# Three new kinds of background step and a re-fitted table of limits in the hand-written schedule of a four-layer attention kernel

## The chip, the cores and the metric

The kernel runs on one core of one Trainium2 chip. The metric is device time in microseconds, the median of three runs; lower is better. A profile of one further execution stands beside it. The core has five engines that matter here: TensorE (PE; its weight loads are listed as PEld), VectorE (DVE), ScalarE (ACT), GpSimd (POOL) and SyncE (SP), which issues the DMAs.

## The reference, cut to what matters

Four layers run one after the other on `x` of 2048 tokens by 512 features, each on a layer norm of `x` and added to `x`. There are 32 heads of 16 features.

```python
x = x + _A_ref(_layernorm(x), ...)   # segments of 512 tokens, causal softmax, plus a memory of earlier segments
x = x + _B_ref(_layernorm(x), ...)   # full softmax attention over 2048 tokens
x = x + _A_ref(_layernorm(x), ...)
x = x + _B_ref(_layernorm(x), ...)
```

In A each of 4 segments computes `softmax(q k^T / 4 + mask) v` inside the segment, blended by a gate with `phi(q) M / (phi(q) z)`, where `M` and `z` sum `phi(k)^T v` and `phi(k)` over earlier segments. In B `softmax(q k^T / 4) v` runs over all keys. Both end with a product with `wo`. Nearly all the work is the exponential of the scores: 2 x 32 x 2048 x 2048 of them in the B layers alone.

## The kernel before, in words

**Units.** Scores are made keys by queries, 128 keys by 512 queries of one head at a time: one *bank*, the size of one of the eight banks of PSUM. A `Group` (from line 328) is one head pair's share of one query segment; `PARTS` (line 324) packs the causal blocks of A into such banks. The main loop, `attention`, takes up to three banks per *unit* (`take_banks`), and `unit` (line 1724) issues their score matmuls (32 rows of PE each, so four can run side by side), then one ACT instruction (line 1801) that takes the exponential of two or three banks at once from PSUM to `pT` in SBUF. Units alternate between two sets of three PSUM banks (`SLOTS`: 0 to 2 and 4 to 6). Two units later `pv_step` multiplies the banks with V (the *sums*), gathered in bank 7 (`SUMS`). All matmuls are recorded at line 622.

**Rings and pairs.** Bank 3 (`MISC`) is the spare one. When `ring_open` or `dx_open` allows it, a unit gives ACT only two banks and sends a third (a *ring*) or a third and a fourth (a *pair*) to VectorE, which computes the exponential in another way: line 1302 (`dx_first`) scales the scores into the bits of a bf16 number, as `uint16`; two *steps* add a constant each (`EXP_STEPS`), giving three tables, and each table is multiplied with V, so such a bank has three products on PE in place of one. Two ring banks make one built buffer, and its steps are a task, `task_dx`: on VectorE at line 1358 (one buffer) or 1391 (two neighbouring buffers at once), or on POOL at line 1373, as `pool_copy` decides. The first step goes to POOL if POOL's estimated end is at most POOL_D after VectorE's (POOL_D of 0: never), the second likewise by POOL_C. `R_PAIRS` is the number of unfinished pairs that still lets a ring open.

**Background.** Everything else is written as generators (`task_A`, `task_mem`, `task_B`, `task_out`): layer norms (lines 795, 824), projections (`proj_fm`, `proj_tm`: four matmuls into bank 3 and an eviction at line 684, or 682 on ACT), output products (line 1140), memory updates, weight loads. A projection may stop half-way (`["cont"]`) and go on after a later unit, and holds bank 3 until then. `background`, called after each unit, runs such steps by `bg_one` while credits (`cr_pe`, `cr_dve`) and the estimated lateness of VectorE (`late`, `EARLY`, `DVE_LATE`) allow; tasks are asked in the order of `make_tasks`, projections by segment. `wide` is set after layer 0's last segment; `near` counts the banks that are ready ahead (`ahead`, up to 400), `low` says that they run short.

**The table.** All of this is decided when the program is built, by estimates (`Sched.estimate`), and nothing on the chip decides. The limits are class constants (from line 445), overridden by `PLAN`, a table whose row k holds for units 20k to 20k + 19 (`STRETCH`, `set_limits`); it has rows 0 to 76.

**Order on the engines.** Each engine runs its own list in order; a wait stops all that is queued behind it on that engine.

Of the kernel before, what the change touches and what calls it, by code (L numbers as in the profile page):

```python
# [362 lines left out]
class Builder:  # L363
# [3 lines left out]
        0: dict(TAKEN_A=1, FILL_DVE=400, MASK_PE=800, PE_LOW=7, GAP=3, BG_BANK=400, QMIN=3, OPART=0, DIV_LATE=2500, PACE=2),  # L367
        1: dict(FILL_DVE=200, MASK_PE=800, GAP=1, BG_BANK=400, QMIN=3, LOW=20, POOL_QM=1, ACT1=600, R_PAIRS=2),
        2: dict(EVAC_ACT=800, NEAR=5, SLACK=350, R_NEAR=10, BACK=6, CARRY_W=400, NEARW=40, OPART=3, PAIRS=60, DIV_LATE=2500, BUSY_WAIT=0, TAKEN=0.3, DVE_LATE=800, BUSY_BACK=800, R_PAIRS=2),
        3: dict(R_LATE=1200, NEARW=40, PAIRS=999, MASK_PE=800, LEVEL=3, TAKEN=0.5, LOW=30, MARGIN=350, TAKEN_A=1, EARLY=300, OPART=3, QUAD=0, FILL=0.47, DX_BANK=900, CR_A=1200, DX_LATE=900, CARRY_W=1500, PART=3, CR_W=2200, HOLD_MAX=0, DVE_LATE=1700, FILL_DVE=100),  # L370
        4: dict(MARGIN=350, DX_BANK=900, NEAR=8, SLACK=550, EARLY=300, FILL=0.42, CR_B=1200, PART=0, NEARW=40, PAIRS=999, BUSY_WAIT=0, DX_FIN=3000, POOL_QM=1, POOL_XN=1, EVAC_ACT=800, R_NEAR=10, BACK=6, CARRY_W=1500, OPART=3, TAKEN=0.3, DVE_LATE=1700, BUSY_BACK=800, LEVEL=3, LOW=30, TAKEN_A=1, QUAD=0, CR_A=1200, DX_LATE=900, PACE=4),
        5: dict(ACT1=400, NEAR=8, TAKEN_A=1, SLACK=550, PV_SKIP=900, FILL_DVE=200, BACK=8, CR_W=1900, NEARW=20, OPART=2, TAKEN=0.4, LOW=14, DVE_LATE=800, QWAIT=8, HOLD_AT=40, PHI_LATE=0, REST=12, POOL_D=2500),
        6: dict(ACT1=400, NEAR=8, TAKEN_A=1, SLACK=550, PV_SKIP=900, FILL_DVE=200, BACK=8, CR_W=1900, NEARW=20, OPART=2, TAKEN=0.4, LOW=14, DVE_LATE=800, QWAIT=8, HOLD_AT=40, PHI_LATE=0, REST=12),
        7: dict(MARGIN=350, R_LATE=1500, DX_LATE=900, TAKEN_A=1, EARLY=300, CARRY_W=1500, PART=3, OPART=3, MASK_PE=800, GAP=3, QUAD=0, QWAIT=3, HOLD_SEGS=2, POOL_XN=1),
        8: dict(R_LATE=1200, NEARW=40, PAIRS=24, MASK_PE=800, LEVEL=3, TAKEN=0.5, LOW=30, MARGIN=350, TAKEN_A=1, EARLY=300, OPART=3, QUAD=0, FILL=0.47, DX_BANK=900, CR_A=1200, DX_LATE=900, CARRY_W=1500, PART=3, CR_W=2200, HOLD_MAX=0, DVE_LATE=1700),
        9: dict(R_LATE=1200, NEARW=40, PAIRS=24, MASK_PE=800, LEVEL=3, TAKEN=0.5, LOW=30, MARGIN=350, TAKEN_A=1, EARLY=300, OPART=3, FILL=0.47, DX_BANK=900, CR_A=1200, HOLD_SEGS=2),
        10: dict(ACT1=400, DX_BANK=700, NEAR=18, BACK=3, CR_W=1900, CR_B=1800, R_PAIRS=2, PAIRS=24, DIV_LATE=800, DVE_LATE=800, POOL_D=2500),
        11: dict(R_LATE=1500, DX_LATE=900, REST=12, NEAR=8, TAKEN_A=1, R_NEAR=50, PV_SKIP=500, FILL_DVE=400, BUSY_ROOM=900, CR_W=1300, DX_LAG=1, LOW=20, HOLD_SEGS=2, BACK=6),
        12: dict(R_LATE=1500, REST=12, NEAR=8, TAKEN_A=1, R_NEAR=50, PV_SKIP=500, FILL_DVE=400, BUSY_ROOM=900, CR_W=1300, DX_LAG=1, LOW=20, HOLD_SEGS=2, BACK=6, PHI_LATE=300),
        13: dict(R_LATE=1500, REST=12, NEAR=8, TAKEN_A=1, R_NEAR=50, PV_SKIP=500, FILL_DVE=400, BUSY_ROOM=900, CR_W=1300, DX_LAG=1, LOW=20, HOLD_SEGS=2, BACK=6, PHI_LATE=300, POOL_D=500, LEVEL=1, POOL_C=4000),  # L380
# [65 lines left out]
    MASK_PE = 500  # L446
    MASK_POOL = 2000
    PHI_LATE = 100
# [3 lines left out]
    NEARW = 60  # L452
# [15 lines left out]
    PART = 2  # L468
# [1742 lines left out]
```

## Time and profile before

| what | value |
|---|---|
| median of 3 runs | 1710.47 us (1709.43 to 1712.46) |
| profiled execution, its time | 1711.88 us |
| its span, first to last instruction | 1710.1 us |
| granted TensorE clock | 0.998 |
| ACT line 1801, instructions | 1543 |
| evictions of ring and pair banks, line 1302 | 1065, of them 107 of two banks |
| steps on VectorE, lines 1358 and 1391 | 373 and 110 (an instruction of line 1391 does two) |
| steps on POOL, line 1373 | 604 |

The span is the profile's own time; some 1.8 us lie outside it. In rows by groups the columns are line, engine, operation, tile written and tile read with shapes, count, busy us, mean ns, and the idle time of the engine before them with what ended it. In rows by windows the columns are the window, its length, then busy us and instruction count of each engine named, the granted clock, and the DMA's share and rate. Matmuls are pipelined, so a busy PE is not PE at its peak. Row k of the table begins with ACT's instruction 20k of line 1801: row 27 at 650.6 us, row 30 at 716.9, row 35 at 829.4, row 58 at 1336.2, row 60 at 1374.1, row 69 at 1546.7.

### The profile page before, as it was taken

To read this page: it belongs to the slowest core of one execution; us is meant where nothing else is said; L and a number is where in the kernel's file an instruction comes from. 1 tells how busy PE (TensorE), PEld (TensorE's weight loads), DVE (VectorE), ACT (ScalarE), POOL (GpSimd) and SP (SyncE) were. 2 spreads that over 40 slices of the span, in tenths; PEclk is the share of its full clock that TensorE was granted. 3 is DMA by queue.
4 is the path that set the end of the run, shared out by engine and by line. 5 is a ranking of instruction groups with operands and counts; after the bars stand their busy time and mean duration, and the time that the engine had idled before them with its cause. 6 is when DMAs were issued, how large, how long until landed. Compare 5 with 4: busy or idle time off the path is not lost.

```text
span 1710.1 us, 45200 instructions
## 1 busy us (share of the span) xinstructions
PE 1607.5 (94%) x19545; PEld 573.2 (34%) x19617; DVE 1456.7 (85%) x2618; ACT 1672.4 (98%) x1590; POOL 838.7 (49%) x944
## 2 busy tenths in 40 slices
PE   8899999999999999999999999999999999999999
PEld 5553435322222233423533522432222222222226
DVE  6657667988999898898688799789899999999996
ACT  8899999999999999999999999999999999999998
POOL 2323112457465464414254144435766766666765
PEclk9999999999999999999999999999999999999999
DMA  6110211000211001221321212012011100100000
GB/s 180 26 33 20 42 17 27 14 14 19 48 32 23 14 11 29 57 54 23 73 60 20 42 48 57 14 20 51 11 20 29 23 10 11 26 11 17 17 14 18
DMA packets 148424, 54.45 MB, mean 32 GB/s; under 512 B 128768, under 2 KB 147712, under 8 KB 148224
## 3 DMA queue, kind: packets, MB, share of 16 engines
q1 hardware_dynamic: 148224, 51.56, 14.2%
q8 instruction: 153, 2.51, 0.6%
q14 instruction: 47, 0.39, 0.1%
HBM read 18.88 MB, written 2.10 MB: 12 GB/s over the span
## 4 chain that ended last, share of the span: by engine, by line
ACT 60%; PE 22%; DVE 13%; POOL 2%; DMA 1%; issue 1%; another core or an unknown queue 0%; ACTq 0%; DVEq 0%; POOLq 0%
ACT pT L1801 58%; PE ps L622 22%; DVE KA L1302 2%; DVE wA L1302 1%; DVE wB L1302 1%; DVE dxt L1302 1%; ACT amem L893 1%; DVE lnst L795 1%; DVE dxt L1358 0%; DVE xn L824 0%; DMA xT<-xn 0%; POOL dxt L1373 0%; DMA phq<-amem 0%; POOL wB L1373 0%; DVE QA L1358 0%
## 5 line engine op out<-in xcount | busy, mean ns | idle before, releaser
L1801 ACT ACTIVATE pT<-ps 128x1024 bf16<-128x1024 f32 (+1 forms) x1543 | 1640.6, 1234 | 25.4 <-PE ps L622 21.0
L622 PE MATMUL ps<-qm,KB 32*128 32x512 bf16 x4096 | 563.8, 384 | 65.5 <-ACT pT L1801 48.9
L622 PE MATMUL ps<-pT,VB 128*17 128x512 bf16 x2849 | 491.5, 384 | 2.8 <-DVE wB L1302 1.2
L622 PEld LDWEIGHTS ps<-qm,KB 32*128 32x128 bf16 x4096 | 144.0, 91 | 585.1 <-ACT pT L1801 464.9
L1302 DVE TENSOR_SCALAR KA<-ps 128x512 uint16<-128x512 f32 (+1 forms) x448 | 319.1, 731 | 18.0 <-PE ps L622 15.3
L1373 POOL TENSOR_TENSOR dxt<-dxt,shift 128x512 int32<-128x512 int32 (+1 forms) x177 | 186.9, 1064 | 261.2 <-DVE dxt L1358 164.2
L1373 POOL TENSOR_TENSOR VA<-KA,shift 128x512 int32<-128x512 int32 (+1 forms) x188 | 193.9, 1040 | 182.6 <-DVE QA L1358 127.2
L1302 DVE TENSOR_SCALAR dxt<-ps 128x512 uint16<-128x512 f32 (+1 forms) x321 | 227.6, 725 | 19.6 <-PE ps L622 17.2
L622 PE MATMUL ps<-dxt,VB 128*17 128x512 bf16 x981 | 212.1, 381 | 0.1
L622 PEld LDWEIGHTS ps<-pT,VB 128*17 128x17 bf16 x2849 | 114.9, 87 | 282.9 <-issue 267.6
L1815 POOL TENSOR_SCALAR_AFFINE_SELECT pT<-pT 128x256 bf16<-128x256 bf16 (+4 forms) x146 | 74.0, 521 | 215.2 <-ACT pT L1801 215.0
L622 PE MATMUL ps<-QA,VB 128*17 128x512 bf16 x465 | 138.7, 382 | 0.4 <-POOL QA L1373 0.3
L622 PE MATMUL ps<-VA,VB 128*17 128x512 bf16 x465 | 127.9, 381 | 0.0
L1373 POOL TENSOR_TENSOR wA<-wA,shift 128x512 int32<-128x512 int32 (+1 forms) x91 | 98.5, 1088 | 53.6 <-DVE wA L1391 19.0
L622 PE MATMUL ps<-KA,VB 128*17 128x512 bf16 x465 | 119.5, 381 | 0.0
L1302 DVE TENSOR_SCALAR wA<-ps 128x512 uint16<-128x512 f32 (+1 forms) x153 | 108.3, 723 | 6.8 <-PE ps L622 6.1
L1302 DVE TENSOR_SCALAR wB<-ps 128x512 uint16<-128x512 f32 (+1 forms) x143 | 109.0, 782 | 5.4 <-PE ps L622 4.2
L1373 POOL TENSOR_TENSOR QA<-KA,shift 128x512 int32<-128x512 int32 (+1 forms) x69 | 77.5, 1129 | 66.5 <-DVE KA L1302 66.4
L622 PE MATMUL ps<-qm,KA 32*128 32x128 bf16 (+2 forms) x1536 | 97.1, 255 | 13.2 <-ACT pT L1801 10.8
L622 PE MATMUL ps<-VA,pT 128*128 128x51 bf16 (+1 forms) x2504 | 104.8, 188 | 2.1 <-DVE ob L1898 1.2
L622 PE MATMUL ps<-wB,VB 128*17 128x512 bf16 x498 | 104.5, 381 | 0.3 <-POOL wB L1373 0.2
L622 PE MATMUL ps<-woB,zero 128*32 128x512 bf16 (+1 forms) x322 | 104.3, 381 | 0.3
(173 smaller groups left out, 2166.0 us busy)
## 6 DMA issues: line engine op xcount, KB each, us to landing
wB<-in_B_wqkv_dram SPq DMA_DIRECT2D x48, 128.0 KB, 2.2
wA<-in_A_wk_dram SPq DMA_DIRECT2D x16, 128.0 KB, 2.3
wA<-in_A_wq_dram SPq DMA_DIRECT2D x16, 128.0 KB, 2.3
wA<-in_A_wv_dram SPq DMA_DIRECT2D x16, 128.0 KB, 2.3
out_dram<-x SPq DMA_DIRECT2D x8, 256.0 KB, 2.2
x<-in_A_x_dram SPq DMA_DIRECT2D x3, 512.0 KB, 10.1
wB<-in_B_wqkv_dram SPq DMA_DIRECT2D x1, 1536.0 KB, 13.1
oT<-ob SPq DMA_TRANSPOSE x63, 2.5
```

The costliest lines, as they stand in the source:

```text
L622: self.sc.add("pe", lambda e: e.matmul(out, lhsT, rhs, start=start, stop=stop, skip_group_check=True), reads=reads, banks=[(bank, "w", all ...
L795: self.op("dve", (lambda i, t: lambda e: e.bn_stats(st[:, k, i, 0:6], self.x[:, t, :]))(i, t), reads=[self.b_x[t]], writes=[bs], ns=690, p ...
L893: self.op("act", lambda e: e.activation(et, src, ACT.Exp), reads=bsrc, writes=self.b_amem, ns=1023, gap=915)
L1302: self.op("dve", lambda e: e.tensor_scalar(d, o, SCALE * LOG2E * 128, 127.0 * 128 + EXP_BIAS, op0=ALU.mult, op1=ALU.add), writes=self.b_dx ...
L1373: self.op("pool", lambda e: e.tensor_tensor(d, s, c, ALU.add), reads=src + [self.b_shift] + [first] * k, writes=dst, ns=165 + 1.75 * n, ga ...
L1801: self.sc.add("act", (lambda dst, src: lambda e: e.activation(dst, src, ACT.Exp, scale=SCALE))(dst, src), writes=self.b_pT[slot * 3 + i:sl ...
L1815: self.op("pool", (lambda blk, pat: lambda e: e.affine_select(blk, blk, pattern=pat, compare_op=ALU.is_ge, fill=0.0, base=0, channel_multi ...
```

## The change

Three new limits, each with a mechanism, and a table in which 72 of 77 rows differ.

- **HURRY** (row 30 only, 2500): `background` goes on when VectorE has neither credit nor spare time, and then picks from the tasks other than `task_dx`; such a step may be issued while VectorE is estimated up to 2500 ns late.
- **SPARE** (row 60 only, 20): when fewer than 20 banks are ahead, a task with matmuls is ready and no ring or pair opens, `lend_bank` keeps a unit at two banks and lends its third PSUM bank to a projection; it stays lent until that projection's last matmul.
- **ORD** (row 27: 23; rows 58, 69, 70: 3): `sort_tasks` re-orders the tasks while the row holds, moving a B layer's projections against the A layer's.
- **FIT=3** (rows 7 and 35): an existing limit; its second bit runs background steps with matmuls between a unit's scores and the sums.
- In the rest of the table limits of all kinds go up and down. R_PAIRS is 2 in 52 rows (41 before). POOL_D above 1 stands in 37 rows (20 before). POOL_D above 1 together with POOL_C of 1500 or more stands in rows 4, 15, 16, 17, 34 to 37, 40, 41, 45, 48, 53 to 56, 58, 70, 74 and 76 (before: 13, 35, 36, 37, 51, 58 and 76). Rows 1 and 2 get PE_LOW=7 and PE_A=6, rows 6 and 7 PE_A=6, row 0 DX_LATE=1700.

```diff
@@ -364,83 +364,83 @@
-        30: dict(ACT1=200, DX_LATE=700, NEAR=10, PV_SKIP=200, EARLY=500, FILL=0.53, CR_B=1800, CARRY_W=1500, OPART=3, DIV_LATE=800, DVE_LATE=800, BG_BANK=100, QUAD=0, LN1_AT=6, FILL_DVE=400, R_LATE=2200, POOL_C=2000, BACK=8, SLACK=250),
...
+        30: dict(ACT1=200, DX_LATE=700, NEAR=10, PV_SKIP=200, EARLY=500, FILL=0.53, CR_B=1800, CARRY_W=1500, OPART=0, DIV_LATE=800, BG_BANK=100, QUAD=0, LN1_AT=6, FILL_DVE=400, R_LATE=2200, POOL_C=0, BACK=8, SLACK=250, REST=4, PAIRS=60, RATE=2, HURRY=2500),
...
-        60: dict(ACT1=300, DX_LATE=900, DX_BANK=700, REST=8, NEAR=3, PV_SKIP=900, BUSY_ROOM=900, FILL=0.47, CR_B=1800, CR_A=1700, PART=3, R_PAIRS=2, NEARW=90, OPART=3, MASK_PE=200, LOW=20, DVE_LATE=800, QWAIT=3, QMIN=4, BACK=2, MARGIN=400),
...
+        60: dict(ACT1=300, DX_LATE=900, DX_BANK=700, REST=8, NEAR=3, PV_SKIP=900, BUSY_ROOM=900, FILL=0.47, CR_B=1800, CR_A=1700, PART=3, R_PAIRS=2, NEARW=90, OPART=3, MASK_PE=200, LOW=20, DVE_LATE=800, QWAIT=3, QMIN=4, BACK=2, MARGIN=400, SPARE=20, PHI_LATE=300),
...
@@ -460,6 +460,10 @@
     PACE = 0
+    SPARE = 0
+    ORD = 0
+    HURRY = 0
+    half_bank = None
...
@@ -699,6 +703,8 @@
     def misc(self):
         pool = self.misc_banks
+        if not self.bubble:
+            return min((self.banks[i] for i in pool), key=self.wait_of)
...
@@ -864,6 +870,7 @@
         bank, al = self.misc(), self.new_alloc()
+        self.half_bank = bank
...
@@ -871,12 +878,14 @@
                          [bw[ci]] + self.b_xT[slot], al)
+        self.half_bank = None
...
     def proj_tm(self, w, bw, off, slot, ti, evac, need=()):
...
         bank, al = self.misc(), self.new_alloc()
+        self.half_bank = bank
...
@@ -884,6 +893,7 @@
                          [bw[ci], self.b_xT[slot][ti]], al)
+        self.half_bank = None
...
@@ -1129,6 +1139,7 @@
             bank, al = self.misc(), self.new_alloc()
+            self.half_bank = bank
...
@@ -1137,6 +1148,7 @@
                 self.mm_wide(bank, a[:, ti * 128:(ti + 1) * 128], wo[:, c, :], n == 0, n == len(srcs) - 1, list(ba) + [bwo], al)
+            self.half_bank = None
...
@@ -1429,7 +1441,7 @@
     def bank_late(self, now=None):
...
-        return self.wait_of(self.misc_bank) - (self.sc.t["pe"] if now is None else now)
+        return min(self.wait_of(self.banks[i]) for i in ([self.misc_bank.idx] if self.bubble else self.misc_banks)) - (self.sc.t["pe"] if now is None else now)
...
@@ -1467,11 +1479,11 @@
-    def bg_one(self, slack=None, bank=None):
+    def bg_one(self, slack=None, bank=None, poor=False):
...
         pick = None
-        if bank is not True and (self.gap > 1 and self.step % 2 or self.dx_urgent()):
+        if bank is not True and not poor and (self.gap > 1 and self.step % 2 or self.dx_urgent()):
...
@@ -1486,11 +1498,11 @@
                 pick = task
-        if pick is None and bank is not True:
+        if pick is None and bank is not True and not poor:
             pick = self.dx_next()
-        if pick is None or (slack is not None and pick["next"][2] > 0 and self.cr_dve + slack < pick["next"][2] and self.late("dve") > self.EARLY):
+        if pick is None or (slack is not None and pick["next"][2] > 0 and self.cr_dve + slack < pick["next"][2] and self.late("dve") > (self.EARLY if pick in self.dx_tasks else max(self.EARLY, self.HURRY))):
             return False
-        if slack is not None and not pick["next"][1] and (pick["next"][2] or not self.PACE) and self.late("dve") > (self.DVE_LATE_LOW if self.low else self.DVE_LATE if not self.ends(1) else self.DVE_FIN):
+        if slack is not None and not pick["next"][1] and (pick["next"][2] or not self.PACE) and self.late("dve") > max(self.DVE_LATE_LOW if self.low else self.DVE_LATE if not self.ends(1) else self.DVE_FIN, 0 if pick in self.dx_tasks else self.HURRY):
...
@@ -1521,8 +1533,9 @@
     def background(self, bank=None):
-        while (self.cr_dve > 0 or self.late("dve") < self.EARLY) and (self.cr_pe > 0 or self.FIT and self.wide and not self.low):
-            if not self.bg_one(self.SLACK, bank):
+        while self.cr_pe > 0 or self.FIT and self.wide and not self.low:
+            poor = not (self.cr_dve > 0 or self.late("dve") < self.EARLY)
+            if poor and not self.HURRY or not self.bg_one(self.SLACK, bank, poor):
...
@@ -1538,10 +1551,16 @@
                     order.append((-5, self.task_out(B, s)))
+        self.first_key = {base * 100 + s * 10 + (13 if base or s > 1 else 5): base * 100 + s * 10 for base in (0, 2) for s in range(4)}
...
         order += [(1000, self.task_dx())]
-        self.tasks = [{"gen": g, "next": next(g)} for _, g in order]
+        self.tasks = [{"gen": g, "next": next(g), "key": k} for k, g in order]
...
+    def sort_tasks(self):
...
+        move = lambda k: self.first_key.get(k, k - self.ORD) + self.ORD
+        self.tasks.sort(key=lambda t: (move(t["key"]), t["key"]) if self.ORD else (t["key"], 0))
...
@@ -1721,9 +1740,18 @@
-    def unit(self, n, items, dx):
+    def lend_bank(self, n, pair):
...
+        bank = self.slot(n)[2 - 2 * (n % 2)]
+        if bank is self.half_bank:
+            return bank
+        if not n or self.bubble or pair or self.near >= self.SPARE:
+            return None
+        return bank if any(t["next"][1] > 0 and self.met(t["next"][0]) for t in self.tasks) else None
...
+    def unit(self, n, items, dx, lent=None):
         pair7 = len(dx) == 2 and self.misc_bank.idx == SUMS
-        u = self.slot(n)[1 if dx and n % 2 and not pair7 else 0:]
+        u = self.slot(n)[1 if (dx and not pair7 or lent is not None) and n % 2 else 0:]
...
@@ -2077,6 +2105,7 @@
         self.stretch = -1
+        self.ordered = 0
...
@@ -2089,12 +2118,18 @@
                 self.set_limits(self.stretch)
+                if self.ORD != self.ordered:
+                    self.sort_tasks()
+                    self.ordered = self.ORD
...
                 self.step -= 1
-            items = self.take_banks(2 if pair else 3)
+            lent = self.lend_bank(n, pair)
+            if lent is not None and lent is self.half_bank:
+                pair = 0
+            items = self.take_banks(2 if pair or lent is not None else 3)
...
@@ -2111,7 +2146,7 @@
                 continue
-            self.misc_banks = [self.misc_bank.idx]
+            self.misc_banks = [self.misc_bank.idx] + ([lent.idx] if lent is not None else [])
...
@@ -2124,7 +2159,7 @@
             dx = []
-            while len(items) == 2 and len(dx) < pair:
+            while len(items) == 2 and lent is None and len(dx) < pair:
...
@@ -2134,7 +2169,7 @@
                     self.ring_step = self.step
-            elif pair:
+            elif pair and lent is None:
...
@@ -2142,7 +2177,7 @@
                 items += self.take_banks(3 - len(items))
-            self.unit(n, items, dx)
+            self.unit(n, items, dx, lent)
```

More of the change, by code (lines that the diff above doesn't have):

```diff
@@ L366 @@
     PLAN = {
[L367 to L370, printed above, removed]
@@ L444 @@
+        76: dict(DX_LATE=700, REST=8, SLACK=700, R_NEAR=20, R_PAIRS=2, NEARW=90, PAIRS=999, LEVEL=1, LOW=14, GAP=1, DVE_LATE=800, BG_BANK=400, QUAD=0, POOL_WAIT=300, PV_SKIP=100, BACK=6, FILL=0.47, PART=0, LN1_AT=3, EARLY=300, DIV_LATE=2500, MARGIN=400, POOL_C=4000, ACT1=300, MASK_PE=200, POOL_D=2500, BUSY_ROOM=300, CR_W=1500, TAKEN=0.5, POOL_XN=1, CR_A=1700, CR_LOW=2000),
     }
```

135 lines of the change are left out of this document (69 added, 66 removed).

## Prediction

> **What bounds the kernel now.** I read the busy times first, then the chain, then ACT's instructions by form, then busy times by stage.
>
> ```profile
> PE 1607.5 (94%) x19545; PEld 573.2 (34%) x19617; DVE 1456.7 (85%) x2618; ACT 1672.4 (98%) x1590; POOL 838.7 (49%) x944
> ```
> ```profile
> ACT 60%; PE 22%; DVE 13%; POOL 2%; DMA 1%; issue 1%; another core or an unknown queue 0%; ACTq 0%; DVEq 0%; POOLq 0%
> ```
> ```profile
> L1801 ACT ACTIVATE pT<-ps 128x1024 bf16<-128x1024 f32 x1065 | 1016.5, 1114 | 8.5 <-PE ps L622 5.8
> L1801 ACT ACTIVATE pT<-ps 128x1536 bf16<-128x1536 f32 x478 | 680.6, 1501 | 16.9 <-PE ps L622 15.2
> ```
> ACT is busy 1672.4 of 1710.1 us, almost all of it in the exponentials of line 1801, which wait only 25.4 us in all. So the kernel ends earlier only if ACT gets fewer score banks (or if the first stage starts ACT sooner). 1065 units have two banks on ACT and 478 have three: 3564 banks. A two-bank unit sends its third bank through VectorE (line 1302), whose steps then run on VectorE (1358, 1391) or POOL (1373). In all 3564 + 1065 + 107 (the wide forms of line 1302 take two) = 4736 banks are fixed by the reference and the masks.
>
> What is a bank worth? I compare a stretch of two-bank units with one that is nearly all three-bank:
>
> ```profile
> 945.00:975.00 30.00, 26.90 (x22) 1.00 0.14 28
> 1604.20:1641.00 36.80, 36.54 (x41) 1.00 0.06 12
> ```
> These are ACT's line 1801 alone. The upper window holds 20 units in 26.9 us (one of two banks), the lower 40 units in 36.5: 1.35 and 0.91 us a unit, with the instructions cut at the edges counted into the 22 and 41. **A bank taken off ACT is worth about 0.41 us** (1501 - 1114 gives 0.39, 1.35 - 0.91 gives 0.44).
>
> Who limits how many banks leave ACT? The stages, each row PE, PEld, DVE, ACT, POOL:
>
> ```profile
> 0.00:300.30 300.30, 272.15 (x3893) 134.95 (x3928) 205.64 (x476) 281.01 (x231) 72.14 (x130) 0.99 0.22 50
> 300.30:611.80 311.50, 295.99 (x3230) 87.37 (x3234) 280.20 (x462) 307.90 (x301) 180.04 (x191) 1.00 0.12 23
> 611.80:801.30 189.50, 178.84 (x2137) 60.50 (x2138) 167.17 (x321) 188.68 (x184) 77.06 (x94) 1.00 0.16 36
> 801.30:1217.10 415.80, 394.64 (x5060) 152.54 (x5080) 343.84 (x653) 409.29 (x372) 185.27 (x213) 1.00 0.19 41
> 1217.10:1710.10 493.00, 465.87 (x5241) 137.84 (x5241) 459.79 (x710) 485.48 (x509) 324.24 (x317) 1.00 0.08 18
> ```
> VectorE is at 90% in the second stage, 93% in the last, but 88% and 83% between. POOL is nowhere over 66%. So where rings are dense VectorE is nearly used up while POOL has room.
>
> **The change, part by part.** Its three new kinds of step hardly run; the table does.
>
> *Lending a bank* needs SPARE, which only row 60 has (units 1200 to 1219, 1374 to 1393 us now), and fewer than 20 banks ahead. *ORD* stands in rows 27, 58, 69 and 70.
>
> ```profile
> L684 DVE CAST KB<-ps x32: 675/691/693, 113.4 to 1219.6; 128x512 bf16<-128x512 f32 x32
> L684 DVE CAST QB<-ps x32: 658/691/692, 115.6 to 1230.2; 128x512 bf16<-128x512 f32 x32
> ```
> The last K and Q projections are done at 1219.6 and 1230.2 us. From then on every group's inputs exist, so 343 units' banks are ahead at row 60, and lending never opens; and in rows 58, 69 and 70 no projection is left whose place ORD could change. In row 27 (651 to 671 us) it puts layer 3's first projection behind layer 2's third segment, which matters only if layer 2's first segment is already through; the order is put back 20 units later. I cost these at zero, and at 2 us either way if the stages have moved. The new `misc()` chooses among one bank outside the start, so zero as well.
>
> *HURRY* stands in row 30, *FIT=3* in 7 and 35 (in 7 it changes nothing, since steps sit between scores and sums there anyway until `wide`).
>
> ```profile
> 716.90:737.10 20.20, 19.07 (x212) 5.52 (x213) 18.45 (x37) 20.20 (x21) 7.57 (x8) 1.00 0.18 51
> 829.40:855.70 26.30, 25.30 (x321) 11.38 (x321) 20.13 (x36) 25.76 (x24) 7.64 (x7) 1.00 0.26 42
> ```
> ACT is busy all 20.20 us of row 30, so HURRY has no idle time to take back; a projection half whose eviction queues up to 2.5 us behind VectorE's other work holds the spare bank, and nobody else needs it in those 2.5 us except a ring. Bounds -1 to +2.5 us, taken as zero. Row 35 has 0.54 us in which ACT is idle; FIT=3 can win that and can lose about as much by putting matmuls ahead of the sums. Zero.
>
> *The early rows* 0 to 2, 6 and 7 give more background work to a unit (PE_LOW 7, PE_A 6).
>
> ```profile
> ACT pT L1801 <- PE ps L622: 10.7, 19, 1.9
> ```
> That is ACT's wait for scores in the first 142.5 us. More projection work per unit brings the next segment sooner and delays these scores; -3 to +5 us, taken as zero.
>
> *The other limits.* 72 of 77 rows change. Two kinds have a direction that can be counted. R_PAIRS is 2 in 52 rows, in 41 before, which lets a ring open with one more pair unfinished. And both steps of a built pair may go to POOL: POOL_D above 1 (first step) together with POOL_C of 1500 or more (second) stands in 20 rows after and 7 before, 13 more. What this does is seen in rows 35 to 37, which have both now, against rows 61 to 63, which have not. In turn for POOL's steps, VectorE's and VectorE's double ones:
>
> ```profile
> 829.40:900.20 70.80, 30.27 (x28) 1.00 0.24 52
> 1392.70:1450.30 57.60, 29.55 (x29) 1.00 0.05 11
> ```
> ```profile
> 829.40:900.20 70.80, 1.66 (x3) 1.00 0.24 52
> 1392.70:1450.30 57.60, 5.85 (x9) 1.00 0.05 11
> ```
> ```profile
> 1392.70:1450.30 57.60, 9.04 (x12) 1.00 0.05 11
> ```
> POOL takes 28 of 31 steps in the first window, 29 of 29 + 9 + 2 x 12 = 62 in the second: 90% against 47%. A row has some 62 / 3 = 21 steps there, 10 in the first window; at 15 a row, 13 more rows move 13 x 15 x 0.43 = 84 steps.
>
> ```profile
> L1358 DVE TENSOR_SCALAR QA<-KA x112: 278/420/1257, 322.4 to 1694.5; 128x1024 uint16<-128x1024 uint16 x107, 128x512 uint16<-128x512 uint16 x5
> ```
> ```profile
> L1373 POOL TENSOR_TENSOR VA<-KA,shift x188: 611/1038/1489, 312.3 to 1696.4; 128x512 int32<-128x512 int32 x181, 128x256 int32<-128x256 int32 x7
> ```
> ```profile
> L1302 DVE TENSOR_SCALAR KA<-ps 128x512 uint16<-128x512 f32 x406 | 269.7, 681 | 14.9 <-PE ps L622 12.2
> ```
> Each frees 0.42 us of VectorE (35 us) and costs POOL 1.04 (87 us, off the path while POOL keeps up: 838.7 + 87 is 54% of the span). A further bank on VectorE costs it 0.68 for the eviction and about 0.12 for its share of the steps, so 35 us pay for 44 banks, 18 us of ACT. Not all comes back: of the added rows those in the second and last stages (15 to 17, 53 to 56, 70, 74) sit where VectorE limits; the others (4, 34, 40, 41, 45, 48) mostly where it had time left. I take somewhat under half: **20 banks, 8 us**. The rest of the table has no sign that I can read from the trace, zero, with 5 us either way.
>
> The sum: 1711.9 us, the profiled execution (span 1710.1 and 1.8 around it), less 8 is 1703.9. The median of the runs is 1710.5, 1.4 lower, so **1702.5 us** as a median.
>
> **The rivals.**
>
> *Slower: POOL's steps lock VectorE out.* The same work on VectorE's SBUF-to-SBUF steps, next to a POOL step and alone:
>
> ```profile
> 704.03 1.04 POOL L1373 TENSOR_TENSOR wB<-wB,shift 128x512 int32<-128x512 int32 x1
> ```
> ```profile
> 704.09 1.26 DVE L1358 TENSOR_SCALAR QA<-KA 128x1024 uint16<-128x1024 uint16 x1
> 705.27 0.41 DVE L1358 TENSOR_SCALAR VA<-KA 128x1024 uint16<-128x1024 uint16 x1
> ```
> The one that began 0.06 us after POOL's took 1.26 us and the next 0.41: it stood still until POOL was done, 0.85 us lost. The Trainium skill, SBUF — State Buffer, section "SBUF: two separate sides", states the rule: the pair of ports that VectorE and GpSimd share is an exclusive lock held for a whole instruction, and the loser blocks; by that rule every step moved can cost VectorE more than it frees, and the trace's 1.26 agrees that the block is whole. The mechanism decides once a moved step costs VectorE over 0.42 us by blocking others. At 0.65 (between 0.42 and 0.85) VectorE loses 84 x 0.23 = 19 us net, 24 banks go back to ACT, +10 us: **1720 us**. Against it:
>
> ```profile
> 1217.10:1710.10 493.00, 67.56 (x121) 1.00 0.08 18
> ```
> ```profile
> 1217.10:1710.10 493.00, 286.46 (x274) 1.00 0.08 18
> ```
> In the last stage 121 single steps on VectorE (upper row) took 67.56 us, 18 more than at 0.41 each, beside 274 POOL steps (lower row): 0.07 us lost for each, far under 0.42. But other VectorE work without PSUM is blocked too, and a reordered table shifts more than these.
>
> *No difference.* The freed VectorE time falls where rings are kept shut by something else (the spare bank is held by a projection, or PE), or one stretch gives back what another wins. This is also the case in which the change does not do what its name says. 1710 us.
>
> *Much faster.* The limits open rings in the middle stages:
>
> ```profile
> L1801 ACT ACTIVATE pT<-ps 128x1024 bf16<-128x1024 f32 x231 | 221.2, 1095 | 3.1 <-PE ps L622 2.5
> ```
> ```profile
> L1801 ACT ACTIVATE pT<-ps 128x1024 bf16<-128x1024 f32 x214 | 207.4, 1062 | 4.1 <-PE ps L622 2.9
> ```
> Two-bank units of the second stage (231 of its 301) and of the fourth (214 of 362). At 18 and 15 of 20 they would be 271 and 272: 98 banks, 40 us; half of that, 20 us, gives **1690 us**. For it: VectorE's 17% of idle time in the fourth stage. Against it: PE is busy 394.6 of 415.8 us there, and a bank on VectorE needs three products with V instead of one, and the spare bank is shared with the projections.
>
> **How the numbers follow.** Forecast 0.52, much faster 0.18, no difference 0.08, slower 0.22. The forecast's own spread, from the zeros with bounds, is 1697 to 1707. The range leaves out half of the much-faster case and somewhat under half of the slower one: 1689 to 1718. Faster by over 0.2% (3.4 us, about what a measurement of this kernel can tell from no change) 0.70, within 0.08, slower 0.22.
>
> **What would show it.** Right: more than 1065 two-bank units (about 1085), POOL busy by about 80 us more, steps of lines 1358 and 1391 fewer by some 80, evictions of line 1302 more by 20, VectorE's share still near 85%, ACT's wait before line 1801 near 25 us. Wrong: the same number of two-bank units with a different time (then it is ACT's waits or the first stage), or mean durations of line 1358 well above 0.51 us with fewer rings (the lock). No unit with two banks on ACT and no bank on VectorE means that lending never ran. If the early stage moves by more than 5 us, my zero for it was wrong.

## The result and the profile after

The kernel after takes **1706.2 us** (median of 20 runs, 1702.1 to 1711.0), the kernel before beside it 1710.3 us (20 runs, 1708.1 to 1713.0): a ratio of **0.9977, 95% interval 0.9968 to 0.9987**. The change makes the kernel about 4 us faster, half of the 8 us that were forecast. The profiled execution of after took 1705.5 us with a span of 1703.8.

From here on lines of the score and sum matmuls are 626 in after (622 before), the exponentials 1829 (1801), ring evictions 1314 (1302), VectorE's steps 1370 and 1403 (1358, 1391), POOL's steps 1385 (1373). The kernels of the experiments have lines of their own.

First the page of after: busy times, and the shares of the chain.

```profile
PE 1603.3 (94%) x19699; PEld 570.6 (33%) x19699; DVE 1472.4 (86%) x2555; ACT 1656.1 (97%) x1574; POOL 966.7 (57%) x1057
...
ACT 53%; PE 26%; DVE 16%; POOL 3%; issue 1%; DMA 0%; ACTq 0%; SPq 0%; POOLq 0%; DVEq 0%
```
ACT is busy 16.3 us less than before, but the span is only 6.3 us shorter: ACT's idle time went from 37.7 to 47.7 us. The chain spends less of the span on ACT (60% before) and more on PE and VectorE (22% and 13%). VectorE, which the change was to relieve, is busier than before.

ACT's exponentials by form:

```profile
L1829 ACT ACTIVATE pT<-ps 128x1024 bf16<-128x1024 f32 x1064 | 1016.4, 1098 | 16.9 <-PE ps L626 14.6
L1829 ACT ACTIVATE pT<-ps 128x1536 bf16<-128x1536 f32 x465 | 660.6, 1503 | 18.8 <-PE ps L626 16.9
```
There are as many two-bank units as before (1064 for 1065), but 13 fewer units of three banks: ACT takes 2 x 1064 + 3 x 465 = 3523 banks, 41 fewer. They left by pairs: 1529 units hold 4736 banks, so 4736 - 3523 - 1064 = 149 units sent a fourth bank to VectorE, against 107. The wait ahead of the exponentials grew from 25.4 to 35.7 us, in both forms.

The first and the last stage (columns as in the prediction's table of stages):

```profile
0.00:300.30 300.30, 273.43 (x3963) 133.30 (x3964) 207.07 (x470) 285.01 (x234) 82.05 (x141) 1.00 0.22 50
...
1217.10:1703.80 486.70, 460.94 (x5235) 139.11 (x5232) 453.23 (x651) 470.88 (x484) 375.21 (x364) 0.99 0.09 18
```
In the first 300.3 us ACT is busy 285.0 us for 281.0, 4.0 us more. So the account of the two profiled executions is: 16.3 us of ACT work removed, 4.0 us of idle time won at the start, and 14.0 us of new idle time later. Not all of the 4.0 is the change's: the trace of before grants PE half the clock twice in this stage, for 3.4 us each at 44 and 68 us, the trace of after not once. In two later runs with before's plan and no such window there (e6 and e10) ACT is busy 283.5 and 283.4 us, so the change's own part is 1.5 us or less.

Who holds up the weight loads, which come ahead of every matmul (columns: who waits for whom, us in total, times, longest):

```profile
PEld ps L626 <- DVE KA L1314: 20.7, 46, 1.6
PEld ps L626 <- DVE dxt L1314: 18.6, 44, 0.9
PEld ps L626 <- DVE wA L1314: 9.8, 20, 1.2
...
PEld ps L626 <- DVE wB L1314: 8.0, 18, 0.9
```
The same in before:

```profile
PEld ps L622 <- DVE KA L1302: 14.0, 37, 1.2
PEld ps L622 <- DVE dxt L1302: 12.7, 32, 1.0
PEld ps L622 <- DVE wB L1302: 7.0, 16, 1.0
PEld ps L622 <- DVE wA L1302: 5.8, 16, 0.7
```
57.1 us on ring and pair evictions; before it was 39.5. So the new waits are for VectorE, and the timeline shows how one arises:

```profile
809.20 2.17 POOL L1385 TENSOR_TENSOR dxt<-dxt,shift 128x512 int32<-128x512 int32 x2 [0.96 <-DVE dxt L1314]
...
809.39 1.00 DVE L1025 TENSOR_TENSOR Mn<-M,hmask 128x128 bf16<-128x128 f32 x1
...
810.42 1.10 DVE L1025 TENSOR_TENSOR Mn<-M,hmask 128x128 bf16<-128x128 f32 x1
...
811.51 0.68 DVE L1314 TENSOR_SCALAR KA<-ps 128x512 uint16<-128x512 f32 x1
812.12 0.28 DVE L1025 TENSOR_TENSOR Mn<-M,hmask 128x128 bf16<-128x128 f32 x1
...
812.25 0.38 PE L626 MATMUL ps<-qm,KB 32*128 32x512 bf16 x1 [1.18 <-DVE KA L1314]
...
813.53 1.02 ACT L1829 ACTIVATE pT<-ps 128x1024 bf16<-128x1024 f32 x1 [1.40 <-PE ps L626]
```
The same small VectorE operation takes 0.28 us alone and 1.00 and 1.10 beside two POOL steps. The eviction behind it comes late, PE waits 1.18 us for the bank, and ACT then stands idle for 1.40. Both inputs of that operation lie in SBUF; the Trainium skill, SBUF — State Buffer, section "SBUF: two separate sides", names such an operation, against a GpSimd one that reads SBUF, as a case of the lock on the shared ports, and this timeline agrees. The place is easy to read, but most of the time that VectorE loses beside POOL is lost by other operations, as e7 shows.

### The profile page after: what moved, and what is told of

It is laid out like the page before. It is cut to its first block, busy times and chain, and to the rows that moved or that the text cites. A ratio compares the mean times of both kernels' runs of the same rounds, so it can differ in the third digit from the quotient of the medians.

```text
span 1703.8 us, 45449 instructions
## 1 busy us (share of the span) xinstructions
PE 1603.3 (94%) x19699; PEld 570.6 (33%) x19699; DVE 1472.4 (86%) x2555; ACT 1656.1 (97%) x1574; POOL 966.7 (57%) x1057
## 4 chain that ended last, share of the span: by engine, by line
ACT 53%; PE 26%; DVE 16%; POOL 3%; issue 1%; DMA 0%; ACTq 0%; SPq 0%; POOLq 0%; DVEq 0%
ACT pT L1829 52%; PE ps L626 25%; DVE KA L1314 3%; DVE dxt L1314 3%; DVE wA L1314 1%; DVE wB L1314 1%; ACT amem L903 1%; DVE dxt L1370 1%; POOL dxt L1385 1%; DVE lnst L801 1%; POOL QA L1385 1%; DVE x L1152 0%; DVE xn L830 0%; DVE wB L1403 0%; POOL pT L1843 0%
## 5 line engine op out<-in xcount | busy, mean ns | idle before, releaser
L1385 POOL TENSOR_TENSOR dxt<-dxt,shift 128x512 int32<-128x512 int32 (+1 forms) x237 | 252.3, 1074 | 244.1 <-DVE dxt L1370 128.7
L1314 DVE TENSOR_SCALAR KA<-ps 128x512 uint16<-128x512 f32 (+1 forms) x424 | 310.9, 753 | 16.8 <-PE ps L626 15.1
L1314 DVE TENSOR_SCALAR dxt<-ps 128x512 uint16<-128x512 f32 (+1 forms) x341 | 249.8, 749 | 18.4 <-PE ps L626 17.0
L626 PE MATMUL ps<-dxt,VB 128*17 128x512 bf16 x1089 | 235.7, 382 | 0.2 <-POOL dxt L1385 0.2
L1843 POOL TENSOR_SCALAR_AFFINE_SELECT pT<-pT 128x512 bf16<-128x512 bf16 (+4 forms) x134 | 73.9, 563 | 222.7 <-ACT pT L1829 222.7
L1385 POOL TENSOR_TENSOR QA<-KA,shift 128x512 int32<-128x512 int32 (+1 forms) x109 | 119.9, 1107 | 65.6 <-DVE KA L1314 62.4
L1385 POOL TENSOR_TENSOR wB<-wB,shift 128x512 int32<-128x512 int32 (+1 forms) x105 | 110.1, 1059 | 43.9 <-DVE wB L1370 17.8
L626 PE MATMUL ps<-wA,VB 128*17 128x512 bf16 x486 | 113.0, 384 | 0.3 <-POOL wA L1385 0.2
L626 PE MATMUL ps<-wB,VB 128*17 128x512 bf16 x519 | 112.5, 390 | 0.1
L626 PE MATMUL ps<-qm,KA 32*128 32x128 bf16 (+2 forms) x1536 | 95.3, 254 | 13.7 <-ACT pT L1829 10.1
## 6 DMA issues: line engine op xcount, KB each, us to landing
wB<-in_B_wqkv_dram SPq DMA_DIRECT2D x1, 1536.0 KB, 12.8
```

The costliest lines, as they stand in the source:

```text
L626: self.sc.add("pe", lambda e: e.matmul(out, lhsT, rhs, start=start, stop=stop, skip_group_check=True), reads=reads, banks=[(bank, "w", all ...
L1314: self.op("dve", lambda e: e.tensor_scalar(d, o, SCALE * LOG2E * 128, 127.0 * 128 + EXP_BIAS, op0=ALU.mult, op1=ALU.add), writes=self.b_dx ...
L1385: self.op("pool", lambda e: e.tensor_tensor(d, s, c, ALU.add), reads=src + [self.b_shift] + [first] * k, writes=dst, ns=165 + 1.75 * n, ga ...
L1843: self.op("pool", (lambda blk, pat: lambda e: e.affine_select(blk, blk, pattern=pat, compare_op=ALU.is_ge, fill=0.0, base=0, channel_multi ...
```

## The experiments

Two theories stood at first. **R**: VectorE's relief by POOL is what gained, and POOL itself is what took most of it back, by the way of VectorE. **C**: the missing part is TensorE's clock, since the trace of after shows three windows of 3.4 us at a granted clock of 0.50, at 512, 1284 and 1304 us (before has two, at 44 and 68). The second, with the stretch ahead of it (columns as in the table of stages):

```profile
1280.00:1283.00 3.00, 2.39 (x18) 0.64 (x16) 2.60 (x4) 3.00 (x5) 2.92 (x4) 1.00 0.21 42
1283.00:1287.60 4.60, 4.32 (x41) 0.96 (x41) 3.23 (x7) 3.36 (x5) 4.44 (x6) 0.63 0.16 32
```
The granted clock (third figure from the end) is 0.63 over these 4.6 us, which reach a little beyond the window. Theory R was narrowed from run to run, and each expectation says in which form it is meant. In all runs but e4 the plan is held: the same units and banks in the same order, and only what the diff names differs.

**e1, more work for PE in its gaps.** 161 short matmuls more, to keep the clock up.

```diff
-        while room > 64 / 2.4 and sc.activity(at) < self.GAP_FILL:
+        while room > 64 / 2.4 and (sc.activity(at) < self.GAP_FILL or sc.activity(at) + self.surplus < 0.78):
```


> The changed kernel with its plan frozen (same units, banks, steps and waits) and 161 more filler matmuls in PE's estimated gaps, so that fewer windows run at half clock. Theory C (half-clock windows of 3.4 us, three of them in the profile after, cost about 1.4 us per 0.001 of mean granted clock): clock 0.999 to 1.0, median 1702 to 1704 us, ACT's wait before the exponentials down from 35.7 to about 30 us. Rival (the windows are a symptom, the spread has another cause): 1706 us as before, or slower by the fillers' own time.

Measured: 1707.7 us (ratio to before 0.9989, 0.998 to 0.9999), mean clock 0.9966 over its 12 runs, the same as after's. Half-clock windows stayed, at other places. The remedy failed, so this run neither proves nor clears the clock.

**e2, before with 80 steps moved to POOL; e3, after with 103 moved back.** Both in the 15 rows in which the change newly lets both steps go to POOL.

```diff
+    def to_pool(self, k):
+        return self.stretch in (4, 15, 16, 17, 34, 40, 41, 45, 48, 53, 54, 55, 56, 70, 74)
```
```diff
+    def to_dve(self, k):
+        return self.stretch in (4, 15, 16, 17, 34, 40, 41, 45, 48, 53, 54, 55, 56, 70, 74) and k == 0
```


> The kernel before, plan frozen, with 80 single steps of the rows that the change gives POOL both steps in executed on POOL instead of VectorE; no bank leaves ACT. Theory R (the relief pays only through banks that leave ACT): VectorE's busy time down by about 30 us, POOL's up by 85, time within 2 us of 1710. The slower rival of the prediction (POOL's steps lock VectorE out): slower by 5 to 19 us, mean of the steps left on VectorE well above 0.51 us.

> The changed kernel, plan frozen, with the 103 first steps of the 15 added rows executed on VectorE again. Theory R (POOL's relief is what lets 41 banks leave ACT): VectorE 43 us busier, its evictions late, ACT's wait up, 8 to 20 us slower than the changed kernel (1714 to 1726). Rival (the gain is the first stage, 6 us by bank 400, and POOL's part is worth nothing): within 3 us of 1706, or faster because the lock is gone.

Measured: e2 1723.6 us (1.0078, 1.0066 to 1.009), 13 us slower than before. VectorE fell to 1433.9 us, but no bank was moved to it for that, so only the price is seen. The price came by POOL's queue: weight loads waited 24.5 us in all for POOL, 13.5 in before, while the steps left on VectorE (128x1024) took 539 ns, 534 before. So the form of R that expected no price missed, and the time is the slower rival's, but not by its sign.

e3 1725.2 us (1.009, 1.0077 to 1.0103), 19 us slower than after; VectorE rose to 1501.1 us:

```profile
PEld ps L658 <- DVE KA L1346: 30.1, 62, 1.6
PEld ps L658 <- DVE dxt L1346: 22.3, 50, 1.8
PEld ps L658 <- DVE wA L1346: 13.7, 27, 1.4
PEld ps L658 <- DVE wB L1346: 11.3, 25, 1.4
```
77.4 us on evictions for 57.1. Without POOL's larger share the banks of after are carried only with these waits, and after is then slower than before: that half of R holds.

**e4, one limit alone.** HURRY is taken out of row 30, everything else of the change stays.

```diff
-...REST=4, PAIRS=60, RATE=2, HURRY=2500),
+...REST=4, PAIRS=60, RATE=2),
```


> The changed kernel without HURRY in row 30, nothing else edited; the rows behind it then meet other states. The prediction's step (HURRY is worth -1 to +2.5 us): 1705 to 1709 us. Rival F (each row is fitted to the state that the rows before it leave, so any change of path costs far more than the edit itself): the profile up to row 30 is the same, then fewer banks leave ACT or ACT waits longer, 20 us or more slower.

Measured: 1740.5 us (1.0179, 1.0165 to 1.0192). This isn't HURRY's worth. Up to row 30 the units are as in after; behind it the plan is another, 17 banks come back to ACT (3540 for 3523), and ACT's wait ahead of the exponentials is 56.3 us for 35.7. The rows behind row 30 fit the state in which it leaves the plan, as rival F said, so single rows can't be priced one by one.

**e5 and e6, evictions ahead of small VectorE work.** A ring or pair eviction passes up to two operations queued ahead of it that have no part in PSUM, where it depends on none of them and its bank is estimated ready (154 places in after, 144 in before).

```diff
+            if op.ring:
...
+                while i and i > len(new) - HOPS and new[i - 1].raw and place[id(new[i - 1])] > known and ready < new[i - 1].end - new[i - 1].ns + EARLIER:
+                    i -= 1
+            new.insert(i, op)
```


> The changed kernel with its plan as it is (same units, same banks, same steps on the same engines); only the order within VectorE's queue differs: in 154 places an eviction of a ring or pair bank stands one or two places earlier, ahead of operations that read and write SBUF alone. Theory R (what the change gained on ScalarE, 16 us, was given back as 10 us of waiting, because evictions stand in VectorE's queue behind small operations that POOL's longer use makes slow): PE's waits on the evictions fall from 57 us towards 45 or less, ScalarE's wait before the exp line from 35.7 to 30 or less, time 1699 to 1704. Theory C (the waiting comes from half-clock windows of TensorE): the order changes nothing, 1704 to 1708 at a granted clock of 0.996 to 0.998. A third: the passed operations (norms, masks, maps) are what PE waits for next, and the time is 1706 to 1712.

> The kernel before, plan as it is, with the same reordering of VectorE's queue in 144 places. Theory R: the waits on evictions are 39.5 us here, so there is less to gain than in the changed kernel: 1706 to 1710. Theory C: 1708 to 1712, no change. Third: 1711 to 1716.

Measured: e5 1707.6 us (0.9983, 0.9974 to 0.9992), e6 1711.1 us (1.0008, 0.9999 to 1.0017). In e5 the waits on evictions fell from 57.1 to 52.0 us, not to 45, and ACT's wait ahead of the exponentials stayed at 35.6. As far as these places reach, the order in VectorE's queue isn't the cause; R in this form fell.

**e7 and e8, POOL's steps cut short.** 16 columns in place of 512 or 256; TensorE reads the first table three times, so the exponential's other two tables are left out of the result.

```diff
-        self.op("pool", lambda e: e.tensor_tensor(d, s, c, ALU.add), ...
+        self.op("pool", lambda e: e.tensor_tensor(d[:, 0:16], s[:, 0:16], bcast(self.shift[:, k:k + 1], [[0, 16]]), ALU.add), ...
...
-        self.pv(g, what, r, self.dx_buf(slot, k)[:, 512 * i:512 * i + 512]...
+        self.pv(g, what, r, self.dx_buf(slot, 0)[:, 512 * i:512 * i + 512]...
```


> The changed kernel with its plan as it is (same units, banks, steps, engines, orders and waits), with every POOL step cut from 256 or 512 columns to 16; TensorE reads the first table in place of the two later ones, so the output leaves out the exponent's last two tables. It prices POOL's steps: VectorE's lengthening beside them and tables or qm that come late from POOL. Theory R, in its form with POOL as the cause (the waits that the change added come from VectorE's operations that stretch beside POOL's steps, and from POOL's queue): 1688 to 1698, ScalarE's wait before the exp line under 28, and the gain against the changed kernel is larger than the same cut gives the kernel before. Theory P (TensorE is simply full in four-bank units): 1703 to 1707, wait still 33 to 37.

> The kernel before with the same cut of POOL's steps. Theory R: 1702 to 1707, ScalarE's wait 18 to 22: it gains about half of what the changed kernel gains, since it has 604 steps against 722 and 39 us of waits on evictions against 57. Theory P: 1708 to 1711, wait 24 to 26.

Measured: after falls to **1677.4 us**, before to **1698.2 us** (the unchanged kernel before, run beside them, 1709.9). By their intervals each is good to about 3 us. The pages of e7 and e8, and e7's exponentials by form:

```profile
PE 1579.4 (94%) x19699; PEld 560.5 (33%) x19699; DVE 1403.2 (84%) x2555; ACT 1648.4 (98%) x1574; POOL 372.0 (22%) x1057
```
```profile
PE 1603.2 (94%) x19617; PEld 567.3 (33%) x19617; DVE 1406.8 (83%) x2618; ACT 1668.3 (98%) x1590; POOL 341.1 (20%) x944
```
```profile
L1872 ACT ACTIVATE pT<-ps 128x1024 bf16<-128x1024 f32 x1064 | 1014.7, 1146 | 2.2 <-PE ps L658 1.2
L1872 ACT ACTIVATE pT<-ps 128x1536 bf16<-128x1536 f32 x465 | 664.7, 1515 | 11.5 <-PE ps L658 10.0
```
This is the account that was missing (the trace of before has 603 steps on POOL, not the 604 of the table ahead):

| | before | after |
|---|---|---|
| POOL's steps | 603 | 722 |
| VectorE busy, steps in full length, us | 1456.7 | 1472.4 |
| VectorE busy, steps short, us | 1406.8 | 1403.2 |
| VectorE stretched by them, us | 49.9 | 69.2 |
| time, steps in full length, us | 1709.9 | 1706.2 |
| time, steps short, us | 1698.2 | 1677.4 |
| price of POOL's steps, us | 11.7 | 28.8 |

What the change does apart from this is worth 1698.2 - 1677.4 = 20.8 us, and 28.8 - 11.7 = 17.1 us of it go to a dearer POOL. With short steps PE is as full as ever (94%), and yet ACT's wait ahead of the exponentials falls to 13.7 us, for 35.7, so a full PE isn't the cause. (Of the 28.6 us by which the spans of after and e7 differ, 20.9 are idle time of ACT and 7.7 busy time; why its busy time falls no run shows.) The weight loads' waits for evictions fall to 27.8 us in e7 (24.1 in e8):

```profile
PEld ps L658 <- DVE dxt L1346: 10.1, 28, 0.6
...
PEld ps L658 <- DVE KA L1346: 7.6, 21, 0.5
PEld ps L658 <- DVE wA L1346: 5.3, 13, 0.9
PEld ps L658 <- DVE wB L1346: 4.8, 12, 0.9
```
Which operations stretch is seen by comparing after with e7, VectorE's groups:

```profile
L1314 DVE TENSOR_SCALAR KA<-ps 128x512 uint16<-128x512 f32 (+1 forms) x424 | 310.9, 753 | 16.8 <-PE ps L626 15.1
...
L1370 DVE TENSOR_SCALAR dxt<-dxt 128x1024 uint16<-128x1024 uint16 (+1 forms) x117 | 67.6, 586 | 1.5
```
```profile
L1346 DVE TENSOR_SCALAR KA<-ps 128x512 uint16<-128x512 f32 (+1 forms) x424 | 313.8, 756 | 28.2 <-PE ps L658 25.6
...
L1402 DVE TENSOR_SCALAR dxt<-dxt 128x1024 uint16<-128x1024 uint16 (+1 forms) x117 | 48.6, 423 | 1.5
```
The evictions from PSUM take 753 and 756 ns, so they aren't touched; the steps from SBUF to SBUF take 586 beside POOL's steps and 423 without. Of 79 us by which VectorE's durations differ in sum, 59 lie in these steps (those of 128x1024 and 128x2048), 9 in the 128x512 bf16 TENSOR_SCALAR and only 1.5 in the small operation of the timeline above.

Short steps also end the waits for tables that come late from POOL, and the clock was higher (a mean of 0.9990 in e7's four runs, against 0.9966). So one more pair.

**e9 and e10, late tables taken away alone.** POOL's steps have their full length, but TensorE reads the first table and doesn't wait for them (the other two tables are left out of the result).

```diff
-                    if w is op or w.eng == "pe" and e == "pe" and not w.is_dma:
+                    if w is op or w.eng == "pe" and e == "pe" and not w.is_dma or e == "pe" and w.step:
```


> The changed kernel with its plan as it is and POOL's steps in full length, but TensorE reads the first table in place of the two later ones and doesn't wait for POOL's steps; the output leaves out the exponent's last two tables. It separates the two ways in which POOL's steps can cost the 28.8 us that cutting them short gave back: by tables that come late from POOL, or by VectorE's operations that stretch beside them. Late tables: most of the 28.8 us comes back, 1677 to 1688, while VectorE stays at 1472 us of busy time. Stretch (VectorE 1472 against 1403 us with short steps): little comes back, 1699 to 1706, at most the 7 us that weight loads wait for POOL's tables; ScalarE's wait before the exp line stays over 28.

> The kernel before with the same: TensorE reads the first table and doesn't wait for POOL's steps. Cutting the steps short gave back 11.7 us here. Late tables: 1698 to 1703. Stretch (VectorE 1457 against 1407 us): 1705 to 1710, at most the 5 us that weight loads wait for POOL's tables.

Measured: e9 1708.6 us (0.9987, 0.9976 to 0.9999), e10 1712.8 us (1.0011, 1.0003 to 1.002). Nothing came back in either; VectorE stood at 1471.4 us in e9, and the weight loads still waited for it:

```profile
PEld ps L658 <- DVE KA L1346: 20.5, 51, 1.6
PEld ps L658 <- DVE dxt L1346: 19.2, 46, 0.9
...
```
With the other two rows they are 60.1 us. Late tables are out, and so is POOL's other work (masks and the like): weight loads waited 12.8 us for it in after and 12.3 in e7. Of the ways in which POOL's steps could cost 28.8 us, two are left: the stretch of VectorE, and the clock, which was as low in e9 (a mean of 0.9959) as in after.

**e11, each POOL step in two halves.** The whole computation; each step is now two shorter instructions.

```diff
+        h = n // PIECES
+        c = bcast(self.shift[:, k:k + 1], [[0, h]])
+
+        def pieces(e):
+            return [e.tensor_tensor(d[:, i * h:i * h + h], s[:, i * h:i * h + h], c, ALU.add) for i in range(PIECES)][-1]
```


> The changed kernel with its plan as it is and the whole computation; every POOL step is issued as two instructions of half the columns (128x256 int32 took 0.61 to 0.67 us in the profiled run, 128x512 1.07 to 1.11), so that what VectorE can be held up at one stroke is halved, and POOL is busy some 90 to 120 us longer. Stretch, if an operation of VectorE waits for the end of the POOL instruction that is under way: what it loses goes with the count times the square of the duration, 2 x 0.63 squared against 1.08 squared, so 69 us of stretch become about 47, VectorE falls from 1472 towards 1450, and about a third of the 28.8 us comes back: 1694 to 1702. Rival: the stretch goes with POOL's busy time, however it is cut: VectorE stays at 1472 or rises to 1480, time 1706 to 1714.

Measured: 1729.6 us (1.0119, 1.0102 to 1.0136): slower, outside both expectations. The page and the waits of the weight loads:

```profile
PE 1603.7 (93%) x19630; PEld 572.7 (33%) x19699; DVE 1459.9 (85%) x2555; ACT 1658.7 (96%) x1574; POOL 1084.1 (63%) x1779
```
```profile
PEld ps L627 <- POOL dxt L1390: 16.9, 24, 1.4
...
PEld ps L627 <- POOL wA L1390: 10.5, 15, 1.7
PEld ps L627 <- POOL wB L1390: 10.3, 12, 2.6
...
PEld ps L627 <- POOL VA L1390: 8.1, 14, 1.2
...
PEld ps L627 <- POOL QA L1390: 5.8, 15, 0.9
```
The stretch did shrink, from 69 to 57 us, about half of what was expected. But POOL became 117 us busier, and where its queue was full its tables came late: 51.6 us of waits for 7.0. Stretch by stretch of 20 units the trace shows both signs: 33 to 36 (POOL busy 24 to 68% in after) took 2.8 us less than in after, while 15, 71 and 75 (74 to 99%) took 8.9 us more.

**e12, halves only where POOL has room.** As e11, in 15 stretches. They were picked by the result of e11: those that were shorter there than in after and left POOL room.

```diff
+SPLIT = {10, 11, 18, 26, 27, 33, 34, 35, 36, 43, 44, 46, 50, 60, 65}
...
+        m = 2 if self.stretch in SPLIT else 1
```


> The changed kernel, whole computation and plan as it is; POOL's steps are issued in two halves only in the 15 stretches of 20 units (some 127 of 722 steps) in which splitting all of them shortened the stretch and left POOL room: 10, 11, 18, 26, 27, 33 to 36, 43, 44, 46, 50, 60 and 65. In the run that split every step these 15 together took 7.0 us less than in the changed kernel's profiled run, while the stretches with POOL busy over 85% lost more than that. Stretch at one stroke, with POOL's queue as the limit where it is full: 1698 to 1703, weight loads waiting for POOL's tables under 12 us. Rival: the 7.0 us were pauses shifted from one stretch to the next, and come back in the stretches after: 1704 to 1709.

Measured: **1700.1 us** (five runs, 1699.2 to 1700.6; 0.9939, 0.9925 to 0.9952), faster than both kernels. The page, the exponentials by form, and the place of the timeline above:

```profile
PE 1591.7 (94%) x19630; PEld 568.9 (34%) x19699; DVE 1461.0 (86%) x2555; ACT 1655.3 (97%) x1574; POOL 992.3 (58%) x1186
```
```profile
L1836 ACT ACTIVATE pT<-ps 128x1024 bf16<-128x1024 f32 x1064 | 1015.4, 1097 | 12.8 <-PE ps L627 10.7
L1836 ACT ACTIVATE pT<-ps 128x1536 bf16<-128x1536 f32 x465 | 660.3, 1502 | 16.5 <-PE ps L627 14.6
```
```profile
807.66 2.50 POOL L1391 TENSOR_TENSOR dxt<-dxt,shift 128x256 int32<-128x256 int32 x4 [0.21 <-DVE dxt L1315]
...
807.85 0.57 DVE L1026 TENSOR_TENSOR Mn<-M,hmask 128x128 bf16<-128x128 f32 x1
...
809.53 0.68 DVE L1315 TENSOR_SCALAR KA<-ps 128x512 uint16<-128x512 f32 x1
...
810.27 0.39 PE L627 MATMUL ps<-qm,KB 32*128 32x512 bf16 x1 [0.61 <-DVE KA L1315]
...
811.55 1.94 ACT L1836 ACTIVATE pT<-ps 128x1024 bf16<-128x1024 f32 x2 [0.83 <-PE ps L627]
```
VectorE is busy 11.4 us less than in after, and ACT's wait ahead of the exponentials falls from 35.7 to 29.3 us. At the place shown the operation that took 1.00 us takes 0.57, PE waits 0.61 us for 1.18 and ACT 0.83 for 1.40. In the profiled runs the 15 stretches took 5.1 us less than in after and the other 62 together 0.8 less, so the pauses weren't shifted but gone. VectorE's part lies in the same 15 stretches: there it is busy 295.4 us for 305.2, in the others 1165.5 for 1167.2. In e11, where the others were split too, VectorE was busy 1165.4 us in them and POOL 892.2 for 800.5: there the halves cost POOL time and freed next to nothing.

## Why the prediction was right, and where it wasn't

Faster was right, and the time lies 3.7 us from the forecast, within the range. That it came so near is in part luck: the sum behind it was wrong in two terms that partly cancel, twice the banks and a price of POOL's steps that it put at nothing.

- **ACT bounds, a bank is worth 0.41 us.** Right: 41 banks took 16.3 us off ACT's busy time, 0.40 each. With short steps the two kernels differ by 20.8 us, of which 41 x 0.41 = 16.8 are banks.
- **Steps moved to POOL.** Well sized. VectorE's step instructions fell from 373 + 2 x 110 to 328 + 2 x 93 steps, 79 fewer, for 84 forecast. POOL got 119 more, since the added banks bring steps of their own, and 128 us, for 87.
- **"I take somewhat under half: 20 banks, 8 us."** This step failed in size: the change took 41 banks, close to the 44 that the freed time pays for. The cut for rows "where it had time left" wasn't needed. They also went by another way than the signs named: pairs, with the number of two-bank units unchanged. That sign, which I had put down as one of a wrong forecast, says nothing about how many banks leave; the count of banks does.
- **The lock.** This rival didn't decide, but it was priced in the wrong coin. VectorE lost 19.3 us more for 119 more steps, 0.16 us a step, well under the 0.42 that I gave as the point at which it decides. As lost VectorE time that would be 19.3 / 0.80 = 24 banks, 10 us; and the forecast had no term for it at all. POOL's steps cost 17.1 us more than before, not as banks (those stayed off ACT) but as waits: an eviction that comes late holds up PE, and PE holds up ACT, as at 809 us. Some 3 of the 17.1 go with the clock (below). "ACT's wait before line 1801 near 25 us" failed by this: 35.7.
- **VectorE's share near 85%** came out at 86, but the 19 us of stretch are in it. With short steps it is 3.6 us below that of before.
- **SPARE, ORD and `misc()` at zero.** Right: with ORD and SPARE taken out of the table the program is the same, instruction for instruction and wait for wait. The spare-bank and re-ordering code never acts.
- **HURRY and FIT at zero.** In row 7 FIT changes nothing, as forecast: the program without it is the same. HURRY and row 35's FIT do change the program, and their worth stays open, since e4 shows that a row can't be taken out alone.
- **The early rows at zero, -3 to +5.** Near enough. The start won 4.0 us between the two profiled executions, under the 5 us at which the zero was to count as wrong, and 1.5 us or less where neither has a half-clock window. (Which sign of -3 to +5 means a gain isn't said.) ACT's wait for scores in the first 142.5 us fell from 10.7 to 7.6, and it is 8.8 in e6 and 8.4 in e10:

```profile
ACT pT L1829 <- PE ps L626: 7.6, 18, 1.8
```
- **No difference, much faster.** Neither came. PE, which I held against the much faster case, isn't what stopped it: the same units at the same 94% ran in 1677.4 us when VectorE wasn't held up.

The sum with the measured terms: 20.8 us gained apart from POOL's steps, less 17.1 for dearer ones, is 3.7; measured 4.1. This closes by its making, since both terms are differences of the same four times. What it can be held against are the 16.8 us of banks and up to 4.0 us at the start, 17 to 21 us for 20.8; and each price is good to about 3 us.

What stays open: how much of the 28.8 us is clock. Over after's 20 runs the time falls by about 1.4 us for each 0.001 of mean granted clock, and short steps raised that mean by 0.0024, so some 3 us go with it; before's mean is 0.9986 with short steps and was 0.9987 in the 23 runs beside e10, so there nothing does. The traces bound it too. Of the 28.6 us by which the spans of after and e7 differ, 6.2 lie in the three stretches of 20 units that hold after's half-clock windows, and 22.4 in the others, where the clock was full in both but for the last microseconds. So most of the price isn't clock. Whether the windows follow from the waits isn't shown: in the 3.4 us ahead of each of after's three, PE stood idle for 0.8 to 1.1 us, about 0.2 being its mean, which fits; the one run that was to part the two, e1, left the windows in place.

## What to carry to other kernels

Work given to POOL isn't free because POOL has room: time the same kernel with POOL's instructions cut short, and compare VectorE's busy time, before you count the relief. Look for the price in the waits of the engine behind VectorE rather than in VectorE's share. Where POOL has slack (24 to 70% busy in the stretches of e12), try its long instructions in two halves; where its queue is full, leave them whole. e12's stretches were picked by a run, so slack alone hasn't been tried as the rule.

## What the hardware showed that I had not expected

- Evictions from PSUM don't stretch beside POOL's steps (753 ns and 756), while SBUF-to-SBUF steps (586 and 423) and small operations with two inputs in SBUF (1.00 to 1.10 us and 0.28) do.
- A POOL step of half the columns takes more than half the time (641 ns for 1072), so that splitting every step costs POOL 117 us. Half steps and whole ones, in e11 and in after:

```profile
L1390 POOL TENSOR_TENSOR VA<-KA,shift 128x256 int32<-128x256 int32 x350 | 215.7, 641 | 65.3 <-DVE QA L1371 34.4 <-DVE QA L1409 27.7
```
```profile
L1385 POOL TENSOR_TENSOR VA<-KA,shift 128x512 int32<-128x512 int32 x175 | 186.2, 1072 | 80.2 <-DVE QA L1370 43.1 <-DVE QA L1403 33.8
```
- The granted clock can halve for 3.4 us at a time in the middle of a kernel whose PE is 94% busy, at 44 and 68 us in before, at 512, 1284 and 1304 us in after, at about 1040 and 1252 us in e12. Where it does differs from execution to execution of one plan, so two profiled executions can differ by a few us in a stage for this alone.
